# A fused attention, expert and MLP kernel: sums of a set's end moved and spread, one conversion moved forward

## The chip, the cores and the metric

The kernel runs on one core of one Trainium2 chip. Its engines are TensorE (PE in the profile, PEld its weight loads), VectorE (DVE), ScalarE (ACT), GpSimd (POOL) and SyncE (SP), which here only issues DMAs. Each engine works through its own instructions in order. The metric is the device time of one execution in microseconds.

## The reference, cut to what matters

```
attn = softmax(q_c @ k_c.T / 8) @ v_c               # chunks of 64, float32
x = attn, heads beside each other                   # 2304 tokens x 512
logits = x @ w_gate;  P = exp(logits - max)
8 times: P /= rows + eps;  P /= columns + eps;  P *= N / E
out = sum over 8 experts of P[:, e] * (relu(x @ w1[e]) @ w2[e])     # 512 -> 1024 -> 512
h = out @ w_in                                      # 512 -> 2048
return (h * clip(h + 3, 0, 6) / 6) @ w_out          # 2048 -> 512
```

Everything is float32 to the caller, but `w_in` and `w_out` arrive as float64, which the kernel turns into float32 with integer operations.

## The kernel before, in words

Every float32 factor is cut into a high and a low part (ScalarE rounds the high part, GpSimd or VectorE subtracts it for the low one), and each product is three TensorE passes over such parts. Large products are split further in the manner of Strassen and Winograd: seven products of half-size blocks in place of eight, with sums of blocks before (of weights, of x) and after (of results).

**Phase one** (to about 301 us) does the attention, the gate and expert 0. While it ends, the first weights of the next phase are loaded and cut.

**The steps.** The rest are 108 steps (`slots`), 28 for each of three token ranges ("sets" one to three, experts 1 to 7) and then 8 for each of the three ranges in the MLP (sets four to six). A step has seven positions, one for each product of `ORDER` (line 871 in the profile, results `ha`, `hb`, `hc`); between products TensorE does the second matrix product of an earlier step (line 1011 in sets one and two, lines 1098 and 1107 later). The rows read from the profile use line numbers of the kernel before.

**Side work.** Other work is put at a place (step, position) in a table: `at_slot` at a fixed one, `book` at the first position from a given one on at which the planner's costs of each engine stay under `CAP`. So the code's order, and with it each engine's order, comes out of this table. The side work that the change touches:

- The float64 conversion (`book_cv`): 32 tiles of seven VectorE instructions each (`cv_op`, lines 191 to 206), with a load before and a store after. 25 tiles stand in set one, 7 in set two.
- `book_ahead`: weight sums, cuts and stores of the MLP's first steps (experts' sets 28 to 31), in set two, through two buffers in turn.
- `book_x2`: cutting the MLP's input of a finished token range into parts, through two buffers in turn, and storing each part (`x2_keep`).
- Step 0's own second weights (`raw_load2(0)` and `w2_piece`), loaded and cut when step 0 begins; step 1's first weights (`w1_piece`) cut in step 0 with the low part on VectorE.

**Sums after, sets three to six.** A group of two steps makes seven results m = 1..7, each added by VectorE (line 1119) into its 768 columns of `accM`; in the first group of a set ScalarE writes them instead (line 1117). In a set's last group the seven are combined (`comb`, line 1066, VectorE, both operands and the result in SBUF) and four blocks are sent out (`block_out`). `MS` is the order in which results come, `y` counts the 14 half positions of a group. In a position the code of a step's own sums comes ahead of the side work and of the group's result.

```
    def acc_m(m):
        return ring["acc"][:, m - 1]

    COMB = {2: [(2, 1)], 5: [(3, 5)], 6: [(6, 1), (7, 6), (3, 6), (5, 7)], 4: [(4, 7)]}
```

So behind result 6 four combinations stand in a row, and in each set result m lies at the same place.

## Time and profile before

| | before |
|---|---|
| median of three runs | 2016.98 us (2009.76 to 2021.1) |
| the profiled execution | 2011.85 us |
| its span, first to last instruction | 2009.8 us |
| TensorE busy | 1942.4 us, 97% |
| VectorE busy | 1389.0 us, 69% |
| GpSimd busy | 1147.3 us, 57% |
| mean granted TensorE clock | 0.989 |

The profiled execution's own time is 2.05 us above its span, and 5.1 us under the median of the three runs. Busy time of TensorE is the sum of pipelined matmuls, so it also covers part of what is lost between them. The granted clock is a share of 2.4 GHz; 0.5 of it is 1.2 GHz.

### The profile page before, as it was taken

The page shows a single profiled execution, that of the slowest core. Times are in us where ns is not written, and L with a number is a line of the kernel's source. Part 1 is how long each engine was busy: PE and PEld are TensorE (multiplying, and loading weights), DVE is VectorE, ACT ScalarE, POOL GpSimd, SP SyncE. Part 2 cuts the span into 40 slices and gives each one's busy share as a digit, 9 for nine tenths or more (in the row PEclk, how much of TensorE's full clock was granted, in tenths as well). Part 3 has the DMA queues.
Part 4 walks back from the last instruction along what each step waited for, and adds up shares of the span by engine and source line. Part 5 has one row for each costly group of instructions (what it writes and reads, how often), then busy time and mean ns, then how long its engine had stood idle before and what let it go on. Part 6 is the DMA issues. An engine that isn't in the chain of part 4 may idle for free.

```text
span 2009.8 us, 33618 instructions
## 1 busy us (share of the span) xinstructions
PE 1942.4 (97%) x11709; PEld 1800.9 (90%) x11709; DVE 1389.0 (69%) x2278; ACT 795.6 (40%) x1586; POOL 1147.3 (57%) x997
## 2 busy tenths in 40 slices
PE   7999999999999999999989999999999999989998
PEld 6778787999999999998878999999999999989998
DVE  6554465788878854559775428778888877777767
ACT  3322224544444445444444434333333344444442
POOL 3221335776777755667666546667667645555443
PEclk8999999999999999999999999999999999999999
DMA  9856558777777779999999887899999998978874
GB/s 219 202 160 172 183 194 267 225 224 249 241 240 222 236 265 314 320 328 363 351 359 364 269 285 276 301 294 351 328 337 334 357 328 281 348 247 297 276 251 147
DMA packets 341704, 552.83 MB, mean 275 GB/s; under 512 B 47504, under 2 KB 171552, under 8 KB 341280
## 3 DMA queue, kind: packets, MB, share of 16 engines
q1 hardware_dynamic: 341536, 550.69, 82.7%
q8 instruction: 93, 1.52, 0.3%
q14 instruction: 75, 0.61, 0.1%
HBM read 365.97 MB, written 184.62 MB: 274 GB/s over the span
## 4 chain that ended last, share of the span: by engine, by line
PE 79%; DMA 7%; DVE 7%; POOL 3%; issue 2%; SPq 2%; ACT 2%; DVEq 0%; ACTq 0%; POOLq 0%
PE acc L1011 19%; PE hb L871 15%; PE ha L871 10%; PE o L1107 10%; PE hc L871 10%; PE o L1098 7%; PE h L546 3%; PE acc L580 3%; DMA wsc<-m 2%; DVE accM L1066 1%; POOL SS L788 1%; DMA q_None<-in_q_dram 1%; DVE accM L1119 1%; SPq L259 1%; DMA r<-in_moe_w_dram 1%
## 5 line engine op out<-in xcount | busy, mean ns | idle before, releaser
L1011 PE MATMUL acc<-W,H 128*128 128x512 f32 x2016 | 519.1, 392 | 10.0 <-POOL H L894 7.2
L1011 PEld LDWEIGHTS acc<-W,H 128*128 128x128 f32 x2016 | 376.0, 188 | 68.0 <-POOL H L894 9.8
L871 PE MATMUL hb<-X,W 128*128 128x384 f32 x1560 | 319.2, 339 | 0.9 <-DVE u L913 0.6
L788 POOL TENSOR_TENSOR W<-r,W 128x512 fp32r<-128x512 f32 x220 | 292.5, 1361 | 9.6 <-DMA r<-in_moe_w_dram 7.2
L871 PEld LDWEIGHTS hb<-X,W 128*128 128x128 f32 x1560 | 276.8, 189 | 13.3 <-DVE u L913 2.2
L871 PE MATMUL hc<-X,W 128*128 128x384 f32 x1200 | 243.6, 338 | 9.5 <-DVE H L888 8.9
L894 POOL TENSOR_TENSOR H<-u,H 128x384 fp32r<-128x384 f32 x112 | 121.1, 1081 | 195.7 <-ACT H L893 172.0
L871 PEld LDWEIGHTS hc<-X,W 128*128 128x128 f32 x1200 | 211.5, 188 | 22.0 <-DVE H L888 12.2
L871 PE MATMUL ha<-X,W 128*128 128x384 f32 x912 | 188.2, 341 | 15.4 <-ACT p L917 14.7
L913 DVE TENSOR_TENSOR u<-hb,p 128x384 f32<-128x384 f32 x216 | 119.6, 554 | 105.5 <-PE hb L871 92.3
L913 DVE TENSOR_TENSOR u<-hc,u 128x384 f32<-128x384 f32 x216 | 119.5, 553 | 101.1 <-PE hc L871 100.6
L871 PEld LDWEIGHTS ha<-X,W 128*128 128x128 f32 x912 | 161.9, 190 | 21.9 <-ACT p L917 16.2
L1119 DVE SCALAR_TENSOR_TENSOR accM<-o,accM 128x768 f32<-128x768 f32 x154 | 147.0, 955 | 48.7 <-PE o L1107 30.3
L892 ACT ACTIVATE u<-u 128x384 f32<-128x384 f32 x112 | 58.8, 525 | 265.7 <-DVE u L913 265.6
L1107 PE MATMUL o<-Hb,W2R 128*128 128x384 f32 x660 | 141.5, 337 | 0.2 <-DMA W2R<-wsc 0.2
L788 POOL TENSOR_TENSOR Hb<-u,Hb 128x384 fp32r<-128x384 f32 x93 | 103.4, 1113 | 59.4 <-ACT Hb L787 49.0
L1098 PE MATMUL o<-W2R,Hb 128*128 128x256 f32 x846 | 130.8, 285 | 0.0
L787 ACT ACTIVATE W<-r 128x512 fp32r<-128x512 f32 x224 | 119.7, 594 | 3.9 <-DMA r<-in_moe_w_dram 3.7
L1098 PEld LDWEIGHTS o<-W2R,Hb 128*128 128x128 f32 x846 | 119.3, 192 | 0.1
L1107 PEld LDWEIGHTS o<-Hb,W2R 128*128 128x128 f32 x660 | 117.7, 188 | 0.4 <-issue 0.4
L1107 PE MATMUL o<-Ha,W2R 128*128 128x384 f32 x516 | 111.7, 336 | 0.0
L546 PE MATMUL h<-xh,w 128*128 128x256 f32 (+1 forms) x384 | 108.5, 349 | 0.0
(190 smaller groups left out, 3578.7 us busy)
## 6 DMA issues: line engine op xcount, KB each, us to landing
W<-wsc SPq DMA_DIRECT2D x504, 256.0 KB, 4.6
W2R<-wsc SPq DMA_DIRECT2D x182, 512.0 KB, 5.3
wsc<-W SPq DMA_DIRECT2D x28, 1792.0 KB, 7.3
r<-in_moe_w_dram SPq DMA_DIRECT2D x112, 256.0 KB, 7.3
wsc<-SS SPq DMA_DIRECT2D x28, 1024.0 KB, 5.9
wsc<-m SPq DMA_DIRECT2D x48, 512.0 KB, 5.6
wsc<-W SPq DMA_DIRECT2D x28, 768.0 KB, 5.4
x2sc<-m SPq DMA_DIRECT2D x42, 384.0 KB, 4.4
```

What stands on the lines that cost most here:

```text
L546: nc.tensor.matmul(out=hps[:, :n], lhsT=w[:, a, kk, :], rhs=xx[:, kk, :], start=(kk == 0 and a == 0 and xx is xh), stop=(kk == KD - 1 and ...
L580: nc.tensor.matmul(out=o[:, :n] if turned else o, lhsT=w[:, a, c] if turned else hx[:, c], rhs=hx[:, :n] if turned else w[:, a, :], start= ...
L787: nc.scalar.activation(out=hi, in_=r, func=AF.Copy)
L788: lo_eng.tensor_tensor(out=lo, in0=r, in1=hi.bitcast(F32), op=ALU.subtract)
L871: nc.tensor.matmul(out=ps[:, :HN], lhsT=W1t[s.b][:, wo, a, kl, :], rhs=x[:, b, kl, :], start=(start and kl == 0 and a == 0 and b == 0), st ...
L892: nc.scalar.activation(out=src, in_=src, func=AF.Relu)
L894: nc.gpsimd.tensor_tensor(out=lo, in0=src, in1=hf, op=ALU.subtract)
L913: nc.vector.tensor_tensor(out=o, in0=ps[b][:, :HN], in1=x, op=ALU.add)
L1011: nc.tensor.matmul(out=o, lhsT=s.Hs[:, fi, hx, t * 128:(t + 1) * 128], rhs=w[:, 0::3, a, :] if fi == 0 else w[:, 1:3, a, :], start=(s.j % ...
L1098: nc.tensor.matmul(out=o[:, t * 256:(t + 1) * 256], lhsT=hs[q][:, b, t * 128:(t + 1) * 128], rhs=w[:, q, a, :], start=(q, a, b) == mm[0], ...
L1107: nc.tensor.matmul(out=ps[:, d, :HN], lhsT=w[:, q, a, d * 128:(d + 1) * 128], rhs=hs[q][:, b, :], start=(q, a, b) == mm[0], stop=(q, a, b) ...
L1119: nc.vector.scalar_tensor_tensor(out=dst, in0=src, scalar=sc, in1=dst, op0=ALU.mult, op1=ALU.add)
```

## The change

What it does, by places in the diff:

1. A set's end: the combinations are bound to half positions `y` instead of results. Five stay on VectorE, three go to GpSimd; (6, 1) is replaced by (7, 1) and (3, 1), which together with (7, 6) and (3, 6) give the same sums. The outputs of blocks 3, 5 and 4 are issued at y = 13 and 14 (the next group's first). `home` puts a new set's results where the old set's come free in the order `FREED`.
2. The float64 conversion: all 32 tiles in set one, from position 9 instead of 12, without the positions left free between instructions, with `CAP` of VectorE at 2.1 instead of 1.95.
3. `book_ahead` in set two starts 4 positions sooner, with 3 positions between cuts instead of 2.
4. `x2_keep` is issued 3 positions behind its cut instead of 2.
5. Step 0's second weights are loaded in phase one (pool `raw2` opens there, `Pb` moves to the other side of SBUF) and cut from position 1; two of step 1's four first-weight cuts have the low part on GpSimd.

```
-    COMB = {2: [(2, 1)], 5: [(3, 5)], 6: [(6, 1), (7, 6), (3, 6), (5, 7)], 4: [(4, 7)]}
-    DONE = {2: [2], 6: [3, 5], 4: [4]}
-    COMB_LAST = {2: [(2, 1)], 6: [(6, 1), (3, 6)], 7: [(7, 6), (4, 7)], 5: [(3, 5), (5, 7)]}
-    DONE_LAST = {2: [2], 5: [3, 5], 4: [4]}
+    V, G = nc.vector, nc.gpsimd
+    ENDS = {
+        MS: ({5: [(G, 2, 1)], 7: [(V, 3, 5)], 9: [(V, 7, 1), (G, 3, 1)],
+              11: [(V, 7, 6), (G, 3, 6)], 12: [(V, 5, 7)], 13: [(V, 4, 7)]},
+             {7: [2], 13: [3, 5], 14: [4]}),
+        MS_LAST: ({3: [(G, 2, 1)], 7: [(V, 6, 1), (G, 3, 6)], 9: [(V, 7, 6), (V, 4, 7)],
+                   11: [(G, 3, 5), (V, 5, 7)]},
+                  {5: [2], 12: [3, 5], 13: [4]}),
+    }
+    FREED = (1, 6, 7, 2, 3, 5, 4)
...
+        if groups[-1].last:
+            home = {m: home[f] for m, f in zip(MS, FREED)}
...
-    def acc_m(m):
-        return ring["acc"][:, m - 1]
-
-    def comb(d, a):
-        nc.vector.tensor_tensor(out=acc_m(d), in0=acc_m(a), in1=acc_m(d), op=ALU.add)
+    def acc_m(g, m):
+        return ring["acc"][:, g.home[m]]
+
+    def comb(g, eng, d, a):
+        eng.tensor_tensor(out=acc_m(g, d), in0=acc_m(g, a), in1=acc_m(g, d), op=ALU.add)
...
+        if y == 0 and n and groups[n - 1].last:
+            close_group(groups[n - 1], 14)
         if g.last:
-            cb, dn = (COMB_LAST, DONE_LAST) if g.ms is MS_LAST else (COMB, DONE)
-            for pair in cb.get(m, ()):
-                comb(*pair)
-            for x in dn.get(m, ()):
-                block_out(g, x)
+            close_group(g, y)
+
+    def close_group(g, y):
+        sums, outs = ENDS[g.ms]
+        for x in sums.get(y, ()):
+            comb(g, *x)
+        for m in outs.get(y, ()):
+            block_out(g, m)
...
-            opened("r", "Pb", 2, "right")
             opened("rr", "raw1", 2, "right")
+            opened("rr", "raw2", 2, "right")
...
+        add(s + 8, 2, raw_load2, 0)
...
-        for name, bufs in (("tmp", 2), ("W11", 1), ("XE", 1), ("M", 1)):
+        for name, bufs in (("tmp", 2), ("W11", 1), ("XE", 1), ("M", 1), ("Pb", 2)):
...
-        raw_load2(0)
...
-        CAP = {"DVE": 1.95, "ACT": 2.4, "POOL": 2.6}
+        CAP = {"DVE": 2.1, "ACT": 2.4, "POOL": 2.6}
...
-                    at_slot(0, z, w1_piece, s, z, nc.vector)
+                    at_slot(0, z, w1_piece, s, z, nc.vector if z > 1 else nc.gpsimd)
...
-            h = book_cuts(g + (1 if s.i else 4), g + 7, [(w2_piece, s, z) for z in range(2)])
+            h = book_cuts(g + 1, g + 7, [(w2_piece, s, z) for z in range(2)])
...
-                    if x in (2, 4):
-                        g += 1
                 at_slot(0, g + 1, cv_keep, i)
-                g = g + 1 if two else max(g + 1, h + 4)
+                g = g if two else max(g + 1, h + 4)
...
-        CV1 = 25
-        g = book_cv(12, list(range(CV1)), True)
+        CV1 = len(cv_list)
+        g = book_cv(9, list(range(CV1)), True)
...
-                at_slot(0, g + 2, x2_keep, p, kl, o)
+                at_slot(0, g + 3, x2_keep, p, kl, o)
...
-        g0 = done[0] + 6
-        book_cv(g0, list(range(CV1, len(cv_list))), False)
+        g0 = done[0] + 2
...
-        g = book_ahead(g0, range(NEXP, FAR), 2, 2)
+        g = book_ahead(g0, range(NEXP, FAR), 2, 3)
```

What this makes of the engines' order, at three places. First VectorE in step 10 of set one, from the step's first sum (`u_10<-hb`) to the weight sums of step 12 (`r_12`); the conversion's instructions are those on `m`. Before:

```order
L913 TENSOR_TENSOR u_10_5063<-hb_5056,p_10_5036 128x384
L198 SCALAR_TENSOR_TENSOR m<-m 128x512
L888 SCALAR_TENSOR_TENSOR H_5035<-ha_5028,H_5035 128x384
L201 TENSOR_SCALAR m<-m 128x512
L913 TENSOR_TENSOR u_10_5102<-hb_5056,p_10_5036 128x384
L770 TENSOR_TENSOR r_12_4986<-r_12_4986 128x256 x3
```

and now:

```order
L913 TENSOR_TENSOR u_10_5101<-hb_5094,p_10_5076 128x384
L204 SCALAR_TENSOR_TENSOR m<-m 128x512
L206 SCALAR_TENSOR_TENSOR m<-m 128x512
L888 SCALAR_TENSOR_TENSOR H_5075<-ha_5068,H_5075 128x384
L191 TENSOR_SCALAR m<-m 128x512
L194 TENSOR_SCALAR m<-m 128x512
L196 TENSOR_SCALAR m<-m 128x512
L913 TENSOR_TENSOR u_10_5145<-hb_5094,p_10_5076 128x384
L770 TENSOR_TENSOR r_12_5022<-r_12_5022 128x256 x3
```

Between the same two sums stand five conversion instructions instead of two, and three of them follow each other directly ahead of the sum that reads `hb` again. In the whole step there are 13 instead of 9, and the last conversion stands in step 22 instead of 26 (of those in set one).

Second VectorE at the end of set three, from the last sum on `hc` before the fourth combination to the differences of step 85 (`t_85`); `accM<-o` is a result added, `accM<-accM` a combination. Before:

```order
L913 TENSOR_TENSOR u_85_15789<-hc_15799,u_85_15789 128x384
L1119 SCALAR_TENSOR_TENSOR accM<-o_5_15792,accM 128x768
L1066 TENSOR_TENSOR accM<-accM 128x768 x4
L949 SCALAR_TENSOR_TENSOR u_85_15789<-u_15810,u_85_15789 128x384
L913 TENSOR_TENSOR p_85_15727<-hb_15739,p_85_15727 128x384
L949 SCALAR_TENSOR_TENSOR p_85_15727<-u_15837,p_85_15727 128x384
L913 TENSOR_TENSOR u_85_15749<-hc_15799,u_85_15749 128x384
L1119 SCALAR_TENSOR_TENSOR accM<-o_6_15840,accM 128x768
L1066 TENSOR_TENSOR accM<-accM 128x768
L949 SCALAR_TENSOR_TENSOR u_85_15749<-u_15857,u_85_15749 128x384
L994 TENSOR_TENSOR t_85_15785<-u_85_15749,t_85_15785 128x384
```

and now:

```order
L913 TENSOR_TENSOR u_85_15791<-hc_15801,u_85_15791 128x384
L1127 SCALAR_TENSOR_TENSOR accM<-o_5_15794,accM 128x768
L1075 TENSOR_TENSOR accM<-accM 128x768
L949 SCALAR_TENSOR_TENSOR u_85_15791<-u_15812,u_85_15791 128x384
L913 TENSOR_TENSOR p_85_15726<-hb_15739,p_85_15726 128x384
L1075 TENSOR_TENSOR accM<-accM 128x768
L949 SCALAR_TENSOR_TENSOR p_85_15726<-u_15835,p_85_15726 128x384
L913 TENSOR_TENSOR u_85_15749<-hc_15801,u_85_15749 128x384
L1127 SCALAR_TENSOR_TENSOR accM<-o_6_15838,accM 128x768
L1075 TENSOR_TENSOR accM<-accM 128x768
L949 SCALAR_TENSOR_TENSOR u_85_15749<-u_15856,u_85_15749 128x384
L994 TENSOR_TENSOR t_85_15787<-u_85_15749,t_85_15787 128x384
```

One combination is left behind result 6 where four were; another now stands behind the sum into `p_85`, and the one behind result 4 has stayed. GpSimd has got, in the same stretch, between the low parts that it cuts (`Ha`, `Hb`):

```order
L788 TENSOR_TENSOR Hb<-u_84_15641,Hb 128x384
L1075 TENSOR_TENSOR accM<-accM 128x768
L788 TENSOR_TENSOR Hb<-t_85_15787,Hb 128x384
L788 TENSOR_TENSOR Hb<-p_84_15579,Hb 128x384
L1075 TENSOR_TENSOR accM<-accM 128x768
L788 TENSOR_TENSOR Hb<-u_85_15791,Hb 128x384
```

These are (3, 1) and (3, 6), which GpSimd did not have before; (2, 1) stands five rows ahead of them.

Third GpSimd at step 0, from the last cut of step 0's first weights (`W_0` from `r_0`, before its number changes) on; `H` are the low parts of step 0's own results. Before:

```order
L788 TENSOR_TENSOR W_0_3045<-r_0_3046,W_0_3045 128x256
L894 TENSOR_TENSOR H_3672<-u_0_3716,H_3672 128x384
L788 TENSOR_TENSOR W_0_3738<-r_0_3661,W_0_3738 128x2x256
L894 TENSOR_TENSOR H_3672<-p_0_3673,H_3672 128x384
L788 TENSOR_TENSOR W_0_3738<-r_0_3661,W_0_3738 128x2x256
L894 TENSOR_TENSOR H_3672<-u_0_3688,H_3672 128x384
```

and now:

```order
L788 TENSOR_TENSOR W_0_3045<-r_0_3046,W_0_3045 128x256
L788 TENSOR_TENSOR W_1_3662<-r_1_3049,W_1_3662 128x2x256 x2
L788 TENSOR_TENSOR W_0_3692<-r_0_3451,W_0_3692 128x2x256 x2
L894 TENSOR_TENSOR H_3672<-u_0_3721,H_3672 128x384
L894 TENSOR_TENSOR H_3672<-p_0_3673,H_3672 128x384
L894 TENSOR_TENSOR H_3672<-u_0_3688,H_3672 128x384
```

The two cuts of the second weights (`W_0_3738` before, `W_0_3692` now) stood between step 0's results and now stand ahead of them, and two cuts for step 1 (`W_1`) have come from VectorE.

## Rows read from the trace of the kernel before

**Rows 1.** The page: TensorE's total, Vector's share in 40 slices.

```profile
PE 1942.4 (97%) x11709; PEld 1800.9 (90%) x11709; DVE 1389.0 (69%) x2278; ACT 795.6 (40%) x1586; POOL 1147.3 (57%) x997
...
DVE  6554465788878854559775428778888877777767
```

**Rows 2.** Whom TensorE waited for, whole execution: sum, times, longest.

```profile
PE ha L871 <- ACT p L917: 14.7, 5, 5.3
PE hc L871 <- DVE H L888: 8.9, 8, 2.8
PE acc L1011 <- POOL H L894: 7.2, 5, 2.8
...
PE acc L1011 <- POOL W L788: 2.0, 1, 2.0
```

**Rows 3.** Four stretches: length; busy PE, PEld, DVE, ACT, POOL; clock.

```profile
315.00:322.00 7.00, 5.63 (x15) 4.85 (x16) 0.56 (x1) 2.02 (x5) 6.67 (x7) 0.52 0.99 366
380.20:442.50 62.30, 62.30 (x313) 56.55 (x313) 50.82 (x74) 27.73 (x56) 44.53 (x37) 1.00 0.75 237
897.00:1105.00 208.00, 192.64 (x946) 169.73 (x945) 152.37 (x220) 88.87 (x177) 148.05 (x117) 1.00 1.01 361
1776.00:1780.00 4.00, 3.57 (x15) 3.57 (x16) 3.28 (x4) 2.60 (x5) 3.92 (x3) 0.57 0.98 299
```

**Rows 4.** Waits of ScalarE from 897 to 1105 us.

```profile
ACT m L787 <- DMA wsc<-m: 60.2, 19, 7.9
```

**Rows 5.** TensorE's order, 1007 to 1013 us: start, us, what.

```profile
1007.40 1.22 PE L871 MATMUL hb<-X,W 128*128 128x384 f32 x6
1008.46 1.52 PE L1011 MATMUL acc<-W,H 128*128 128x512 f32 x6
1012.44 1.31 PE L871 MATMUL hc<-X,W 128*128 128x384 f32 x6 [2.46 <-DVE H L888]
```

**Rows 6.** Vector's groups by line, 380.2 to 442.5 us.

```profile
L770 DVE TENSOR_TENSOR r<-r 128x256 f32<-128x256 f32 x16 | 12.4, 792 | 0.1
...
L204 DVE SCALAR_TENSOR_TENSOR m<-m 128x512 f32<-128x512 uint32 x4 | 4.2, 1051 | 0.0
...
L191 DVE TENSOR_SCALAR m<-m 128x512 uint32<-128x512 uint32 x4 | 1.8, 461 | 0.0
```

**Rows 7.** One Vector line, 335 to 733 us: ns shortest/median/longest.

```profile
L770 DVE TENSOR_TENSOR r<-r x96: 408/416/1502, 342.4 to 704.5; 128x256 f32<-128x256 f32 x96
```

**Rows 8.** The same for a line that reads PSUM.

```profile
L913 DVE TENSOR_TENSOR u<-hb,p x52: 543/558/559, 337.2 to 731.7; 128x384 f32<-128x384 f32 x52
```

**Rows 9.** GpSimd in order of time from 300 us.

```profile
311.88 1.02 POOL L894 TENSOR_TENSOR H<-u,H 128x384 fp32r<-128x384 f32 x1 [19.78 <-DMA r<-in_moe_w_dram]
```

**Rows 10.** Vector in order of time at a set's end.

```profile
1634.90 3.69 DVE L1066 TENSOR_TENSOR accM<-accM 128x768 f32<-128x768 f32 x4
...
1640.27 0.85 DVE L949 SCALAR_TENSOR_TENSOR p<-u,p 128x384 f32<-128x384 f32 x1 [0.74 <-ACT u L944]
...
1642.49 1.15 DVE L1066 TENSOR_TENSOR accM<-accM 128x768 f32<-128x768 f32 x1
```

**Rows 11.** TensorE in order of time: the stops behind ScalarE.

```profile
1645.81 1.42 PE L871 MATMUL ha<-X,W 128*128 128x384 f32 x5 [3.54 <-ACT p L917]
...
1738.64 1.65 PE L871 MATMUL ha<-X,W 128*128 128x384 f32 x4 [2.11 <-ACT p L917]
...
1776.43 1.97 PE L871 MATMUL ha<-X,W 128*128 128x384 f32 x5 [5.35 <-ACT p L917]
```

**Rows 12.** ScalarE in order of time, third set.

```profile
1737.28 0.52 ACT L634 ACTIVATE m<-m 128x384 fp32r<-128x384 f32 x1 [2.80 <-DMA x2sc<-m]
```

**Rows 13.** GpSimd's groups of the whole execution (page).

```profile
L894 POOL TENSOR_TENSOR H<-u,H 128x384 fp32r<-128x384 f32 x112 | 121.1, 1081 | 195.7 <-ACT H L893 172.0
```

**Rows 14.** Vector in order of time at the end.

```profile
2003.04 1.95 DVE L1066 TENSOR_TENSOR accM<-accM 128x768 f32<-128x768 f32 x2
2004.90 0.95 DVE L1119 SCALAR_TENSOR_TENSOR accM<-o,accM 128x768 f32<-128x768 f32 x1
```

More of the change, by code (lines that the diff above doesn't have):

```diff
@@ L1048, in chunk_attention_moe_mlp @@
             ab=(a, b), mlp=s.mlp, p=s.p, at=s.i + 2, first=s.j == 0,
-            last=b.i + 1 in ends, ms=MS_LAST if b is slots[-1] else MS,
+            last=b.i + 1 in ends, ms=MS_LAST if b is slots[-1] else MS, home=home,
         ))
+        if groups[-1].last:
+            home = {m: home[f] for m, f in zip(MS, FREED)}
     ring = {}
@@ L1071, in block_out @@
             nc.sync.dma_start(
-                out=xraw[:, :, i, j, :], in_=acc_m(m).rearrange("p (k n) -> p k n", k=2)
+                out=xraw[:, :, i, j, :], in_=acc_m(g, m).rearrange("p (k n) -> p k n", k=2)
             )
@@ L1410, in chunk_attention_moe_mlp @@
             opened("a", name, bufs, "left")
-        opened("rr", "raw2", 2, "right")
         opened("rr", "sum2", 1, "right")
```

30 lines of the change are left out of this document (15 added, 15 removed).

## The prediction

> **What bounds the kernel now.** I read the page first, then TensorE's waits, then stretches of the span, and last single engines in order of time where TensorE stopped. TensorE is busy for 97% of the span, while VectorE's share varies between 4 and 8 tenths [rows 1]. What can be won is therefore what TensorE loses at its stops, and most of the steps lose nothing: the 62.30 us from 380.2 to 442.5 hold four steps with TensorE busy for all of them, 15.58 us a step and 15.58 / 7 = 2.23 us a position [rows 3]. Here VectorE is busy for 50.82 us, so it has 11.5 us free per four steps. The stops lie at three kinds of places.
>
> *Step 0.* TensorE waits 2.0 us for the low part of a second weight [rows 2], and some smaller waits for results' low parts (1.8 us together, a part of the 7.2 and 8.9 us of [rows 2]) come before it. GpSimd itself had stood for 19.78 us behind a load of weights [rows 9], so its queue runs late. From 315 to 322 the granted clock is 0.52, 1.2 GHz against the 2.4 GHz of a normal stretch [rows 3]: another 7.0 x 0.48 = 3.4 us. Together 7.2 us.
>
> *Set two while the MLP's weights are prepared.* From 897 to 1105 us TensorE is busy for 192.64 of 208.00 us [rows 3]: 15.4 us in ten stops, the longest 2.8 us, nearly all named "low part of a result, GpSimd or VectorE" [rows 2]. Behind them stands ScalarE, which in that stretch waits 60.2 us in 19 waits for a store out of one of `book_ahead`'s two buffers, at most 7.9 us [rows 4]. ScalarE's next cut of a result is queued behind such a wait, the low part behind the cut, and the product that reads it behind that. One stop in order of time: two products begin 1.06 us apart, the next one 3.98 us later, of which 2.46 us are idle [rows 5].
>
> *The set ends.* TensorE stops 3.54 us at the end of set three and 5.35 us at the end of set four [rows 11]; set five's end repeats the first (the five waits on `p` of 14.7 us [rows 2], less the three of [rows 11], leave 3.7 us for it and a small one; I take 3.5). At 1776 to 1780 the clock is 0.57 [rows 3], a further 4.0 x 0.43 = 1.7 us. ScalarE's `p` comes late because VectorE does four combinations in one go, 3.69 us, and a fifth of 1.15 us right ahead of the next step's differences [rows 10]. All three ends cost 12.4 + 3 x 1.7 = 17.5 us.
>
> A last stop of 2.11 us stands alone at 1738.64 [rows 11]: ScalarE had waited 2.80 us for a store of `book_x2` [rows 12].
>
> **The change part by part.** The sum is made against the profiled execution, 2011.85 us (span 2009.8 and 2.05 us around it).
>
> *Step 0.* The second weights' loads move ahead of the first results, their two cuts with them, so the 2.0 us wait has no ground left, and the low clock that follows a stop goes if the stop goes: 2.0 + 3.4 = 5.4 us. Against it, three loads are now on SP's queue ahead of three other issues of phase one, and GpSimd gets two cuts that VectorE did. Below: the 2.0 us alone. Above: all 7.2. **Term: -5.5** (-2 to -7).
>
> *Set two.* With 3 positions between cuts the way from a buffer's store to its next use grows from 2 positions, 2 x 2.23 = 4.5 us, to 4, 8.9 us, and the longest wait was 7.9 us [rows 4]. That would be above every store seen. The conversion's loads and stores leave this stretch as well, and its work starts 4 positions sooner. If all waits go, 15.4 us come back; a wait that stays behind another queue keeps some. **Term: -15** (-12 to -17; a whole failure is a rival below).
>
> *Set ends.* Behind result 6 stand now one combination and not four. VectorE still does five per end, but ahead of the differences only three, spread: 4.84 us before, 3 x 0.92 = 2.8 us now, and the 0.74 us that it stood for `u` behind them [rows 10] goes too: it gets there up to 2.8 us sooner. Three go to GpSimd. It has no such sum in the trace; its nearest row is the low part, 1081 ns for 384 columns [rows 13], so about 2.2 us for 768 (an estimate from that row). What such a sum costs VectorE is shown by a line that adds two operands from SBUF: 416 ns in the median and 1502 at most, and 792 in the mean of the dense stretch [rows 6, 7], while a line with one operand in PSUM takes 543 to 559 ns whatever runs beside it [rows 8]. So one of VectorE's SBUF sums can be held by 1.1 us, and by all of the 2.2 us at worst. Per end that leaves between 0.6 and 2.8 us; taking 2.0 of it, three times: **-6** (0 if the stretch eats it, -17.5 if every stop and its low clock go).
>
> [...]
>
> *`book_x2` one position later.* In the third set a buffer is used again 4 positions on, so its store now has one position less before reuse. The wait that already costs 2.11 us there [rows 11, 12] grows by up to 2.23 us. Other sets use the buffers more slowly, and there the slack covers it. **+2** (0 to +4).
>
> *The tail.* Two combinations and an addition ended the kernel on VectorE, 1.95 + 0.95 us [rows 14]. Now (3, 5) is on GpSimd, about 2.2 us by the estimate above, and (5, 7) must wait until it has read result 5, with the last addition queued behind it. **+1** (0 to +2).
>
> *Set one.* The conversion goes from 28 to 41 instructions per four steps (32 tiles of seven, 224, over about 21.7 steps). Its seven lines take from 461 to 1051 ns [rows 6], 23.5 us for 28, so 0.84 us in the mean; 13 more are 10.9 us in 11.5 free ones [rows 3, 6]. On average they fit, but VectorE is then full to the last per cent, and where three stand in a row, the low part that `hb` or `hc` waits for stands behind 2.5 us of them. Over 21.7 / 4 = 5.4 such cycles the loss is 0 if all fits and 15 us if an instruction costs 1.05 us (13 x 1.05 = 13.7, 2.2 too much, and once more for irregularity); nearer the first, as products come two positions after their cuts. **+4** (0 to +15).
>
> *At nothing:* `home` and `FREED` (an address, no instruction; ScalarE writes a new set's results where the old are out already, and TensorE covers it, busy through), the later outputs (store queues idle then; one would cost its landing, of the size of [rows 4], only if its columns were reused at once).
>
> Sum: -5.5 - 15 - 6 + 2 + 1 + 4 = -19.5, that is 1992.4 us on the profiled execution. The four known times (three runs and the profiled one) have a mean of 2014.9, 3.1 us above it, which I add: **1995 us**.
>
> **The rivals** (times with those 3 us).
> 1. *All stops vanish.* 7.2 + 15.4 + 17.5 + 2.1 = 42.2 us: 1973. For it: each is a short wait behind a named instruction. Against it: set ends need over 5 us and get 2.8.
> 2. *GpSimd's sums hold VectorE for their whole length.* The set ends give nothing, the tail costs 2: 1995 + 6 + 1 = 2002. For it speak the 1502 ns [rows 7].
> 3. *Set two keeps its stops,* because the stores wait for a queue and not for time: the 60.2 us [rows 4] stay, with 4 positions between. 1995 + 15 = 2010, no change to be told. Against it: 7.9 us was the longest.
> 4. *The other side: VectorE becomes the bound of set one.* If an added conversion costs 1.5 us, as the held sum does [rows 7], then 13 x 1.5 = 19.5 us meet 11.5 free ones; 8.0 x 5.4 = 43 us in place of 4: 1995 + 39 = 2034. It decides from the price at which the loss is 23.5 us, 13p = 11.5 + 23.5 / 5.4, p = 1.22 us. For it: the fullest stretch has 45 us of GpSimd beside VectorE [rows 3]. Against it: that 0.84 was measured beside the same GpSimd.
>
> **How the numbers follow.** Chances: the forecast 0.55, rival 1 0.13, rival 2 0.12, rivals 3 and 4 0.10 each. The forecast's own range, terms partly summed, is 1983 to 2005. For 8 in 10 the range takes in rival 1 and rival 2 and rival 3's middle: 1972 to 2012; rival 4 stays out. A change of 0.5% (10 us) is about what this measurement can tell; below 2007 counts as faster. Forecast, rivals 1 and 2 lie there but for 0.03 and 0.02: 0.75, and 0.03 of rivals 3 and 4 where gains elsewhere carry them, so faster 0.78. Same 0.13 (rival 3 and those edges), slower 0.09.
>
> **What would show it.** Step 0: no wait of the second product for a weight's low part, clock 1.0 behind it. Set two: ScalarE's 60.2 us of waits for stores nearly gone, ten stops of TensorE gone. Set ends: stops of 1 to 3 us at the three places, the row of four combinations split, VectorE's SBUF sums longer where GpSimd's stand beside. `book_x2`: a stop of 2 to 4 us in the third set. Set one: steps still 15.58 us; a window of four steps above 62.30 with TensorE waiting for `H` from VectorE would show rival 4, and make the prediction wrong.

## The result and the profile after

The changed kernel takes 2028.66 us in the median of 12 runs (2023.03 to 2033.28), the kernel before 2016.51 us (12 runs, 2009.76 to 2021.1). The ratio is 1.0063, with a 95% interval of 1.0048 to 1.0078: 12 us slower, where 1995 us and a gain were forecast. The profiled execution of the changed kernel has a span of 2021.8 us, 12.0 us above that of the kernel before.

Line numbers of the kernel after differ from those before in the result's part alone: 1107, 1098, 1119, 1066 are now 1116, 1107, 1127, 1075; 1117 is 1125. First the page: TensorE's total, and VectorE's busy tenths in 40 slices.

```profile
PE 1944.4 (96%) x11709; PEld 1798.7 (89%) x11709; DVE 1388.0 (69%) x2267; ACT 794.3 (39%) x1586; POOL 1182.9 (59%) x1011
...
DVE  6554466899999734444454528778888877877766
```

TensorE's work is the same as in [rows 1]. In set one VectorE's slices 9 to 13 have gone from 7 and 8 to 9, which is 90% or more; in set two its slices 19 to 21 from 9, 7 and 7 to 4, 4 and 5. Then TensorE's waits over the whole execution, as sum, times, longest:

```profile
PE ha L871 <- ACT p L917: 18.1, 6, 4.8
PE hb L871 <- DVE u L913: 13.7, 17, 1.9
PE hc L871 <- DVE H L888: 5.7, 4, 2.1
```

The waits of [rows 2] for low parts from GpSimd (7.2 us in five) and for a weight (2.0 us) are gone. A wait that cost 0.6 us before is now the second, 13.7 us in 17, and its releaser is VectorE. The waits for `p` grew from 14.7 to 18.1 us.

Where the 12 us lie is read from when the first product of each step starts (TensorE in order of time). A second profile of the kernel before, taken later, stands beside it:

| from the first product of ... | before | before, again | changed |
|---|---|---|---|
| the start (phase one) | 301.23 | 306.79 | 304.80 |
| steps 0 and 1 | 32.23 | 29.90 | 28.46 |
| steps 2 to 26 (set one) | 389.75 | 389.76 | 416.57 |
| steps 38 to 49 (set two) | 206.56 | 206.59 | 187.56 |
| steps 85 and 86 (end of set three) | 35.67 | 36.78 | 35.79 |
| steps 92 and 93 | 34.55 | 32.73 | 35.83 |
| step 94 (end of set four) | 21.87 | 23.01 | 22.31 |
| steps 101 and 102 (end of set five) | 35.37 | 36.50 | 36.45 |
| step 107 to the end | 36.88 | 36.89 | 37.95 |

Phase one differs by 5.6 us between two executions of one program, so its 3.6 us say nothing of the change. Of the rest set one lost 26.8 us and set two won 19.0 us; everything else together comes to 0.6 us. The loss in set one is itself from one profile: four of the runs below have the same code there, and with theirs it is 25.5 to 31.1 us.

Two stretches of the changed kernel, with the columns of [rows 3]: four steps of set one (13 to 16), and steps 38 to 49.

```profile
522.39:587.93 65.54, 63.62 (x314) 55.97 (x313) 63.80 (x88) 27.71 (x56) 49.12 (x37) 1.00 0.73 232
924.38:1111.94 187.56, 187.56 (x937) 169.55 (x937) 88.25 (x159) 84.37 (x168) 128.85 (x109) 1.00 1.00 345
```

Four steps that took 62.30 us take 65.54, with VectorE busy for 63.80 of them: it has 1.7 us left, where it had 11.5. In set two TensorE is busy for the whole stretch, VectorE for 88 us (152 of 208 before [rows 3]), and ScalarE's wait for the stores out of the two buffers [rows 4] does not appear any more.

VectorE's groups by line from 333 to 687 us, four of them (the last operation of the conversion, the weight sums, then the conversion's sixth and first operation), with count, busy us, mean ns and the idle time before them:

```profile
L206 DVE SCALAR_TENSOR_TENSOR m<-m 128x512 f32<-128x512 f32 x31 | 41.5, 1340 | 0.7
L770 DVE TENSOR_TENSOR r<-r 128x256 f32<-128x256 f32 x84 | 41.2, 506 | 0.5
...
L204 DVE SCALAR_TENSOR_TENSOR m<-m 128x512 f32<-128x512 uint32 x31 | 32.9, 1060 | 13.0 <-DMA scr_in<-m 9.6 <-DMA scr_out<-m 2.8
...
L191 DVE TENSOR_SCALAR m<-m 128x512 uint32<-128x512 uint32 x31 | 25.8, 834 | 0.5
```

L191 took 461 ns before [rows 6] and takes 834; L770 has fallen from 792 to 506. All seven conversion lines together take 1.012 us an instruction (219.6 us for 217 in this stretch), against 0.829 us in steps 2 to 26 of the kernel before (143.4 us for 173).

What an instruction waits for can be read from the trace one by one. Of the 218 conversion instructions in steps 2 to 26 of the changed kernel 139 take over 0.2 us more than the shortest of their line. Each of these 139 ends one such shortest time after the end of a GpSimd instruction (to within 0.15 us), as if it had begun only then, and of the 39 that no GpSimd instruction runs beside none is longer. Their time above the shortest is 104.5 us together. In the kernel before 72 of 172 are longer, by 48.8 us together.

The row of L204 shows something else that the prediction did not have. VectorE waits 12.4 us in eight waits, up to 3.7 us, for a store of the conversion to leave; in the kernel before no such wait is in the trace. L204 writes the buffer that the tile's result is stored from, and there is one such buffer: without the positions left free, the next tile comes to it before the last store has landed.

How the hold reaches TensorE is seen at 559 us, first in VectorE's order, then in GpSimd's and TensorE's:

```profile
558.27 1.13 DVE L194 TENSOR_SCALAR m<-m 128x512 uint32<-128x512 uint32 x1
559.43 1.41 DVE L196 TENSOR_SCALAR m<-m 128x512 uint32<-128x512 uint32 x1
560.87 1.67 DVE L198 SCALAR_TENSOR_TENSOR m<-m 128x512 uint32<-128x512 uint32 x1
562.47 0.54 DVE L913 TENSOR_TENSOR u<-hb,p 128x384 f32<-128x384 f32 x1
```

```profile
558.01 1.11 POOL L894 TENSOR_TENSOR H<-u,H 128x384 fp32r<-128x384 f32 x1 [0.79 <-ACT H L893]
559.08 7.18 POOL L788 TENSOR_TENSOR W<-r,W 128x512 fp32r<-128x512 f32 x5
```

```profile
563.07 1.31 PE L871 MATMUL hb<-X,W 128*128 128x384 f32 x6 [0.42 <-DVE u L913]
```

Three conversion instructions stand in a row ahead of the sum that `hb` waits for. They take 1.13, 1.41 and 1.67 us, 4.2 us together, where a position is 2.23 us long. GpSimd is busy beside all three. So the sum starts late, and TensorE stops for 0.42 us. Of the 17 stops on this sum 15 lie between 345 and 684 us, and three on `hc` beside them, up to 2.1 us each. Four of these 18 stops (5.2 us of 16.6) come 1.6 to 3.0 us behind one of VectorE's waits for a store; no run separates their share.

At the end of set three, GpSimd's combinations, VectorE's next to them, and TensorE's stop:

```profile
1638.40 2.56 POOL L1075 TENSOR_TENSOR accM<-accM 128x768 f32<-128x768 f32 x1
...
1643.18 2.56 POOL L1075 TENSOR_TENSOR accM<-accM 128x768 f32<-128x768 f32 x1
```

```profile
1637.56 1.70 DVE L1075 TENSOR_TENSOR accM<-accM 128x768 f32<-128x768 f32 x1
...
1642.75 1.30 DVE L1075 TENSOR_TENSOR accM<-accM 128x768 f32<-128x768 f32 x1
1643.97 2.20 DVE L949 SCALAR_TENSOR_TENSOR u<-u,u 128x384 f32<-128x384 f32 x1
```

```profile
1653.42 2.15 PE L871 MATMUL ha<-X,W 128*128 128x384 f32 x6 [4.33 <-ACT p L917]
```

These two GpSimd combinations take 2.56 us each (the shortest of the twelve takes 1.80). While a GpSimd instruction runs, a VectorE instruction with two operands from SBUF takes longer, until that one ends: the two combinations took 1.70 and 1.30 us where 0.92 was the mean in [rows 10], beside low parts that GpSimd cuts, and the instruction at 1643.97, beside the second GpSimd combination, 2.20 us instead of 0.55. The stop on `p` is 4.33 us, 3.54 before [rows 11].

At step 0, ScalarE's copy of expert 0's last results, GpSimd's four weight cuts, and VectorE beside them:

```profile
307.35 0.73 ACT L599 ACTIVATE ev<-acc 128x256 f32<-128x256 f32 x2 [2.69 <-PE cp L511]
```

```profile
309.05 5.50 POOL L788 TENSOR_TENSOR W<-r,W 128x512 fp32r<-128x512 f32 x4 [13.38 <-DVE u L913]
```

```profile
309.30 1.08 DVE L520 TENSOR_SCALAR scs<-scs 128x8 f32<-128x8 f32 x1
...
310.65 1.10 DVE L525 TENSOR_TENSOR P<-P,scr 128x144 f32<-128x144 f32 x1
...
312.13 1.29 DVE L788 TENSOR_TENSOR W<-r,W 128x512 fp32r<-128x512 f32 x1
```

The two stops on the second weights are gone. TensorE now waits for `p` (1.20 us), which stands behind the copy at 307.35, and longer for VectorE (1.38, 0.36 and 1.23 us, where 0.40, 0.82 and 0.61 were lost to it before). The wait for `p` is no sure mark of the change: it is 0.44 us in the second profile of the kernel before, and 0.14 us in one of the runs below with the changed step 0 (that with GpSimd relieved). The longer ones come from VectorE's instructions: L520 took 0.17 us before and takes 1.08, L525 0.31 and takes 1.10, the cut 0.68 and takes 1.29, all while GpSimd cuts four pieces in a row.

### The profile page after: what moved, and what is told of

It reads as the page before. It is cut to its first block, busy times and chain, and to the rows that moved or that the text cites. A ratio compares the mean times of both kernels' runs of the same rounds, so it can differ in the third digit from the quotient of the medians.

```text
span 2021.8 us, 33668 instructions
## 1 busy us (share of the span) xinstructions
PE 1944.4 (96%) x11709; PEld 1798.7 (89%) x11709; DVE 1388.0 (69%) x2267; ACT 794.3 (39%) x1586; POOL 1182.9 (59%) x1011
## 4 chain that ended last, share of the span: by engine, by line
PE 71%; DVE 15%; DMA 6%; issue 4%; ACT 1%; SPq 1%; POOL 1%; POOLq 0%; DVEq 0%; ACTq 0%
PE acc L1011 16%; PE hb L871 13%; PE o L1116 10%; PE hc L871 9%; PE ha L871 9%; PE o L1107 7%; PE acc L580 3%; PE h L546 3%; DVE u L913 2%; DMA scr_out<-m 1%; DVE m L204 1%; DVE r L770 1%; DVE m L194 1%; DMA st<-in_moe_w_dram 1%; DVE accM L1127 1%
## 5 line engine op out<-in xcount | busy, mean ns | idle before, releaser
L871 PE MATMUL hb<-X,W 128*128 128x384 f32 x1560 | 320.1, 340 | 13.8 <-DVE u L913 13.7
L788 POOL TENSOR_TENSOR W<-r,W 128x512 fp32r<-128x512 f32 x222 | 302.8, 1393 | 18.1 <-DVE u L913 13.4
L871 PE MATMUL ha<-X,W 128*128 128x384 f32 x912 | 188.4, 342 | 18.8 <-ACT p L917 18.1
L788 POOL TENSOR_TENSOR Hb<-u,Hb 128x384 fp32r<-128x384 f32 x93 | 103.7, 1116 | 49.8 <-ACT Hb L787 44.3
```

What stands on the lines that cost most here:

```text
L788: lo_eng.tensor_tensor(out=lo, in0=r, in1=hi.bitcast(F32), op=ALU.subtract)
L871: nc.tensor.matmul(out=ps[:, :HN], lhsT=W1t[s.b][:, wo, a, kl, :], rhs=x[:, b, kl, :], start=(start and kl == 0 and a == 0 and b == 0), st ...
```

## The experiments

The main theory after the result: GpSimd's instructions hold VectorE's instructions on SBUF (not those that read PSUM, [rows 8]), so each instruction added to VectorE in set one costs more than its own time, and the same holds for the combinations moved to GpSimd. The rival: VectorE's own amount and order of work alone.

**Conversion spread over all of set one.**

```diff
-                    g = book(g, cv_op, i, x, dve=c)
+                    g = book(max(g, 9 + (7 * n + x) * 4 // 5), cv_op, i, x, dve=c)
```

> The changed kernel with its 224 conversion instructions spread evenly over set one, 0.8 of a position apart (35 in four steps, the last in step 26, instead of 41 and step 22). Theory A, VectorE is simply over-full in set one (41 x 1.01 us and the rest ask for more than the 62.3 us of four steps): 35 x 0.9 us fit nearly, the 26.8 us that steps 2 to 26 lost against the kernel before shrink below 6, and the whole is 20 to 26 us shorter than the changed kernel. Theory B, it is not the amount but several conversion instructions standing ahead of one sum: at one or two a position with the weight sums between them the stops stay in part, and at least 12 of the 26.8 us remain.

Measured: 2005.62 us, ratio to the kernel before 0.9955 (0.9940 to 0.9970). Steps 2 to 26 take 400.15 us: 10.4 of the 26.8 us remain, between the two expectations. The stretch from 380 to 660 us:

```profile
380.00:660.00 280.00, 276.38 (x1374) 249.49 (x1373) 245.47 (x353) 123.01 (x251) 200.40 (x157) 0.99 0.76 245
```

VectorE has 34.5 of 280 us free and TensorE still loses 3.6, in stops of 0.6 to 1.8 us on `hb` every 64 us. One of them, VectorE first:

```profile
469.05 0.69 DVE L204 SCALAR_TENSOR_TENSOR m<-m 128x512 f32<-128x512 uint32 x1 [3.71 <-DMA scr_out<-m]
469.78 1.64 DVE L206 SCALAR_TENSOR_TENSOR m<-m 128x512 f32<-128x512 f32 x1
471.34 0.54 DVE L913 TENSOR_TENSOR u<-hb,p 128x384 f32<-128x384 f32 x1
```

```profile
471.94 1.68 PE L871 MATMUL hb<-X,W 128*128 128x384 f32 x6 [1.83 <-DVE u L913]
```

So the amount counts. What is left is not a matter of amount or rows alone: each of the six stops in steps 2 to 26 comes 2.9 to 4.0 us behind a wait of VectorE of 2.2 to 3.7 us for a store of the conversion, and behind the wait stands an instruction that GpSimd holds. No run takes these waits away at this density.

**Conversion as before, the new distances in set two kept.**

```diff
-        CV1 = len(cv_list)
-        g = book_cv(9, list(range(CV1)), True)
+        CV1 = 25
+        g = book_cv(12, list(range(CV1)), True)
...
+        book_cv(done[0] + 6, list(range(CV1, len(cv_list))), False)
         g0 = done[0] + 2
```

with the old free positions and the old cap.

> The changed kernel with the conversion as it was before (25 tiles in set one, 7 in set two, the old distances and the old cap of 1.95), but with the new distances of the weight preparation in set two. Set one: steps of 15.58 us again, about -26 us against the changed kernel by either theory. Set two: if the third position between cuts is what removed ScalarE's 60.2 us of waits for stores, they stay below 10 us and 897 to 1105 loses under 3 us; if it was that the conversion's seven tiles left this stretch (their loads, stores and VectorE work), at least 10 of the 19 us gained there are lost again.

Measured: 2000.47 us, ratio 0.9939 (0.9922 to 0.9956). Set one is back at 389.76 us. Steps 38 to 49 take 189.56 us, 17.0 of the 19.0 us that were won. ScalarE's waits for stores in that stretch:

```profile
ACT m L787 <- DMA wsc<-m: 8.4, 5, 3.4
```

8.4 us in place of 60.2 [rows 4]: `book_ahead`'s own new places are what cured set two (the third position between cuts and the sooner start, which this run keeps both and does not separate); that the conversion left it is worth 2.0 us.

**All combinations on VectorE, at the same places.**

```diff
-        MS: ({5: [(G, 2, 1)], 7: [(V, 3, 5)], 9: [(V, 7, 1), (G, 3, 1)],
-              11: [(V, 7, 6), (G, 3, 6)], 12: [(V, 5, 7)], 13: [(V, 4, 7)]},
+        MS: ({5: [(V, 2, 1)], 7: [(V, 3, 5)], 9: [(V, 7, 1), (V, 3, 1)],
+              11: [(V, 7, 6), (V, 3, 6)], 12: [(V, 5, 7)], 13: [(V, 4, 7)]},
...
```

(The last set's table, `MS_LAST`, is changed in the same way.)

> The changed kernel with the three GpSimd combinations of each set end given to VectorE, at the same half positions. Theory A, a GpSimd sum of 2.56 us holds VectorE's sums with two SBUF operands for its whole length (2.20 us for one that takes 0.55): VectorE reaches the differences of the next step 2 to 3 us sooner, the stops of 4.33, 4.79 and 4.28 us at the three set ends fall to 1 to 3 us, the tail loses the 1.98 us that VectorE waits for GpSimd, and the whole is 5 to 9 us shorter. Theory B, VectorE is late there by its own work: five to eight combinations cost it 0.94 us each, the stops become as long as in the kernel before (3.5 to 5.4 us) or longer, and only the tail's 1 us is won.

Measured: 2025.79 us, ratio 1.0057 (1.0043 to 1.0071), which can't be told from the changed kernel's 1.0063 (1.0048 to 1.0078). The three set ends take 92.61 us together (changed 94.55, before 92.91 and 96.29), the tail 36.89. The stops are 3.33, 4.03 and 3.02 us, above theory A's 1 to 3 and below those of the kernel before. Neither theory holds alone: without GpSimd's combinations VectorE has eight of its own, which are long here too, since GpSimd's low parts run beside them:

```profile
1639.88 2.65 DVE L1075 TENSOR_TENSOR accM<-accM 128x768 f32<-128x768 f32 x2
...
1645.29 2.17 DVE L1075 TENSOR_TENSOR accM<-accM 128x768 f32<-128x768 f32 x2
...
1648.32 0.94 DVE L1075 TENSOR_TENSOR accM<-accM 128x768 f32<-128x768 f32 x1
...
1651.91 1.43 DVE L1075 TENSOR_TENSOR accM<-accM 128x768 f32<-128x768 f32 x1
```

Six combinations, 7.2 us, stand ahead of the differences.

**GpSimd relieved in set one.** ScalarE writes the low parts of the weights as a copy; the subtraction is left out. (The expectation says sets one and two; set two reads these weights ready from memory, so the edit works in set one alone.)

```diff
+        if lo_eng is None:
+            nc.scalar.activation(out=lo, in_=r, func=AF.Copy)
+            return
         lo_eng.tensor_tensor(out=lo, in0=r, in1=hi.bitcast(F32), op=ALU.subtract)
...
```

(The lines left out name the weights of steps 2 to 27.)

> The changed kernel, but in sets one and two the low parts of the weights are written by ScalarE as a plain copy (the subtraction is left out), so GpSimd only cuts results there; VectorE has the same instructions in the same density, 41 conversion instructions in four steps. Theory A, the conversion is dear because GpSimd's instructions hold VectorE's: its mean falls from 1.01 us to 0.6 to 0.75, VectorE has time left, and most of the 26.8 us lost in steps 2 to 26 is gone (20 us or more shorter than the changed kernel). Theory B, VectorE's own work and its order do it: the mean stays over 0.9 us and the steps stay at 15.6, 17.1 and 17.2 us.

Measured: 2003.56 us, ratio 0.9945 (0.9930 to 0.9961). Steps 2 to 26 take 391.75 us: 24.8 of the 26.8 us are gone, with every VectorE instruction in its place. The same three groups and a stretch of 65 us (DVE is the third of the busy times, POOL the fifth):

```profile
L770 DVE TENSOR_TENSOR r<-r 128x256 f32<-128x256 f32 x89 | 35.8, 418 | 0.6
...
L206 DVE SCALAR_TENSOR_TENSOR m<-m 128x512 f32<-128x512 f32 x32 | 22.2, 693 | 0.7
...
L191 DVE TENSOR_SCALAR m<-m 128x512 uint32<-128x512 uint32 x31 | 14.6, 471 | 0.5
```

```profile
515.00:580.00 65.00, 65.00 (x328) 59.03 (x327) 48.42 (x93) 40.35 (x82) 12.79 (x12) 1.00 0.82 267
```

L206 falls from 1340 to 693 ns and L191 from 834 to 471. The mean of the seven lines is 0.61 us. GpSimd is busy for 12.8 us of 65 instead of 49 of 65.5, and TensorE never stops in this stretch. VectorE's waits for the conversion's stores are still there, 23.4 us in eleven, and behind them comes TensorE's only stop of over 0.3 us in set one, 1.17 us. This settles it: the price is GpSimd's, and the waits for stores cost nearly nothing without it.

**The store of `book_x2` 2 positions behind its cut again.**

```diff
-                at_slot(0, g + 3, x2_keep, p, kl, o)
+                at_slot(0, g + 2, x2_keep, p, kl, o)
```

> The changed kernel with book_x2's store again 2 positions behind its cut instead of 3. Theory A, the position taken from the time between store and reuse made the third set's stop longer: the stop at step 92 (3.1 to 3.5 us in the changed kernel and its variants) falls to about 2.1 us, and the stops of 1.06 and 0.95 us that came in step 93 go: 2 to 3 us in steps 92 and 93. Theory B, those stops come from the store's own landing or from another queue: they stay within 0.5 us.

Measured, one run: 2027.04 us. TensorE's stops in steps 92 and 93:

```profile
1751.26 1.44 PE L871 MATMUL ha<-X,W 128*128 128x384 f32 x6 [1.79 <-ACT p L917]
...
1775.40 1.34 PE L871 MATMUL hb<-X,W 128*128 128x384 f32 x6 [1.06 <-DVE u L913]
...
1778.72 1.32 PE L871 MATMUL hc<-XE,W 128*128 128x384 f32 x6 [0.93 <-DVE u L913]
```

The first falls from 3.10 to 1.79 us, as theory A has it, but this profile wins no time by it: step 92 takes 18.37 us (18.16 in the changed kernel). Over all profiles here it takes 18.2 to 20.9 us in the eight with 3 positions, 19.9 in the mean, and 16.7 to 18.7 us in the six with 2, 17.6 in the mean, so the position costs some 2.3 us. The other two stops stay, and are not `book_x2`'s. They are not GpSimd's either: step 93 takes 17.5 us here and 17.98 and 17.96 us in the two runs that have these combinations on VectorE (the one above and that with late combinations), but 15.8 to 16.0 in the kernel before and the joined ones. What only the latter are without is the pair (7, 1) and (3, 1), which stands in step 93; that it is the cause is not shown.

**The old share of the conversion, three at a time.**

```diff
-                    g = book(g, cv_op, i, x, dve=c)
+                    g = max(g, 9 + (7 * n + x) // 3 * 3)
+                    at_slot(0, g, cv_op, i, x)
```

(25 tiles in set one, 7 in set two.)

> The changed kernel with the old share of the conversion in set one (25 tiles, 28 instructions in four steps, as in the kernel before), but placed three at a time in every third position instead of one or two a position; seven tiles follow in set two. Theory A, the loss in set one comes from the amount (VectorE beside GpSimd has no time for 41 of them in four steps): with 28 steps 2 to 26 stay at 389.8 us or lose under 3 us. Theory B, three in a row ahead of a sum are enough by themselves: each third position loses some tenths of a us, 10 to 27 us in all, as in the changed kernel.

Measured, one run: 2038.59 us. Steps 2 to 26 take 402.28 us, 12.5 us more than with the same instructions one or two at a time: theory B, near its lower end. None of VectorE's waits here is for a store of the conversion, so the rows of three do it without them; an instruction takes 0.93 us in the mean (0.83 at one or two a position). In set two the edit puts all seven instructions of a tile into one position, an extreme that was not meant and shows the mechanism best. VectorE, and then TensorE:

```profile
979.43 1.51 DVE L191 TENSOR_SCALAR m<-m 128x512 uint32<-128x512 uint32 x1
...
985.37 1.48 DVE L201 TENSOR_SCALAR m<-m 128x512 uint32<-128x512 uint32 x1
986.89 0.69 DVE L204 SCALAR_TENSOR_TENSOR m<-m 128x512 f32<-128x512 uint32 x1
```

```profile
988.83 1.65 PE L871 MATMUL hb<-X,W 128*128 128x384 f32 x4 [6.81 <-DVE u L913]
```

Seven instructions from 979.43 to 988.22 (five of them held at 1.4 to 1.6 us, the last two free at 0.69) and a stop of 6.81 us on the sum behind them. Steps 38 to 49 take 215.09 us.

**Step 0's second weights loaded sooner.**

```diff
-        add(s + 8, 2, raw_load2, 0)
+        add(s + 3, 2, raw_load2, 0)
```

> The changed kernel with step 0's second weights loaded five half steps sooner in phase one, ahead of the queue that its last stores stand in. Theory A, these loads delay the store out of ScalarE's copy of expert 0's results, and with it the first p of step 0: ScalarE's wait for that store falls from 2.7 to 3.8 us to 1.5 us as before, and TensorE's stop on ha in step 0 (1.2 to 2.3 us) goes; the three stops on VectorE behind it (1.4, 0.4 and 1.2 us) stay, since they come from GpSimd's four weight cuts in a row. Theory B, ScalarE's wait has to do with the 1792 KB store of the first weights alone: the stop on ha stays over 1 us.

Measured, one run: 2024.71 us. ScalarE's copy:

```profile
307.50 0.70 ACT L599 ACTIVATE ev<-acc 128x256 f32<-128x256 f32 x2 [3.93 <-DMA asc_t<-ev]
```

The wait is still 3.93 us and the stop on `ha` 2.41 us. Theory A of this run falls; what delays that store stays open. The three stops on VectorE behind it, which both theories let stand, shrink to one of 0.74 us; why is not shown.

**The late combinations.**

```diff
-        MS: ({5: [(G, 2, 1)], 7: [(V, 3, 5)], 9: [(V, 7, 1), (G, 3, 1)],
-              11: [(V, 7, 6), (G, 3, 6)], 12: [(V, 5, 7)], 13: [(V, 4, 7)]},
-             {7: [2], 13: [3, 5], 14: [4]}),
+        MS: ({5: [(V, 2, 1)], 7: [(V, 3, 5)], 9: [(V, 7, 1), (V, 3, 1)],
+              15: [(V, 7, 6), (V, 3, 6)], 16: [(V, 5, 7), (V, 4, 7)]},
+             {7: [2], 15: [3], 16: [5, 4]}),
...
-        if y == 0 and n and groups[n - 1].last:
-            close_group(groups[n - 1], 14)
+        if n and groups[n - 1].last:
+            close_group(groups[n - 1], 14 + y)
```

> The changed kernel with all combinations of a set's end on VectorE, and the four that need result 6 moved behind the last differences of the old set's last step (half positions 15 and 16, the next group's second and third), with the outputs behind them; the old columns are free before the new results 3 and 2 come. Theory A, what costs at a set's end is that sums with two SBUF operands, GpSimd's or VectorE's, stand ahead of the differences that ScalarE's p is queued behind: the stops of 4.3, 4.8 and 4.3 us fall below 1 us each and the low clock behind them goes, 12 to 18 us. Theory B, the step at the boundary itself (other weights, ScalarE writing the first results) makes the stop: at least 2.5 us of each stay.

(`MS_LAST` goes to VectorE here too, at its old places.) Measured: 2015.26 us, ratio 1.0006 (0.9993 to 1.0020), 0.57% or some 11.5 us below the changed kernel's ratio. The set ends take 32.02, 17.65 and 31.72 us, 13.2 us less together, and the tail 1.1 us less. The clock in these three stretches is 1.00, where the changed kernel has 0.95, 0.85 and 0.91. The waits for `p` in the whole execution:

```profile
PE ha L871 <- ACT p L917: 6.0, 5, 2.9
```

6.0 us in place of 18.1, half of it the one at step 92. Theory A, though a stop of 1.44 us on `hb` has come in step 94.

**Joined.** The conversion as before, the store 2 positions behind its cut, the set ends late with (6, 1) back in place of (7, 1) and (3, 1):

```diff
...
+        MS: ({5: [(V, 2, 1)], 7: [(V, 3, 5)], 14: [(V, 6, 1)], 15: [(V, 7, 6), (V, 3, 6)],
+              16: [(V, 5, 7), (V, 4, 7)]},
+             {7: [2], 15: [3], 16: [5, 4]}),
...
```

> The changed kernel with what the runs spoke for: the conversion as before (25 tiles in set one), book_x2's store 2 positions behind its cut, and the set ends with all combinations on VectorE and five of the seven behind the last differences. If the stages add up without touching each other: set one 389.8 us, set two's stretch 189.6 us, the set ends as in the run with late combinations (14 us under the kernel before together), steps 92 and 93 under 35 us. That is 26 to 30 us below the kernel before, some 1.3 to 1.5%. Rival: the late combinations collide with the cuts of the third set's MLP input, whose stop at step 92 grows and takes back over 5 us.

Measured: 1982.04 us (1981.57 to 1984.34), ratio 0.9845 (0.9830 to 0.9861): 1.5% below the kernel before, some 31 us where 26 to 30 were expected. Set one 390.20 us, steps 38 to 49 189.73, the set ends 31.02, 18.64 and 31.11, steps 92 and 93 32.87, so the rival falls. The last four combinations at the end of set three, and TensorE around them:

```profile
1628.49 2.63 DVE L1075 TENSOR_TENSOR accM<-accM 128x768 f32<-128x768 f32 x2
...
1631.52 2.65 DVE L1075 TENSOR_TENSOR accM<-accM 128x768 f32<-128x768 f32 x2
```

```profile
1635.15 1.31 PE L871 MATMUL hb<-XE,W 128*128 128x384 f32 x6 [0.79 <-DVE u L913]
...
1643.70 1.30 PE L871 MATMUL ha<-X,W 128*128 128x384 f32 x6
```

These four cost VectorE 5.3 us, more than the 4.84 us of the five in [rows 10]. But they stand behind the second and the third difference, and ScalarE's `p` is queued behind its cut of the first: TensorE loses 0.79 us on one product and none on `p`, which stopped it for 3.54 us. The end of set four still stops it for 0.91 us on `p` and 2.39 us on `hb`.

**Step 1's first weights cut on VectorE again**, in the joined kernel:

```diff
-                    at_slot(0, z, w1_piece, s, z, nc.vector if z > 1 else nc.gpsimd)
+                    at_slot(0, z, w1_piece, s, z, nc.vector)
```

and **step 0 wholly as before**, in the joined kernel: the same line, the pools as before, and

```diff
-        add(s + 8, 2, raw_load2, 0)
...
+        raw_load2(0)
...
-            h = book_cuts(g + 1, g + 7, [(w2_piece, s, z) for z in range(2)])
+            h = book_cuts(g + (1 if s.i else 4), g + 7, [(w2_piece, s, z) for z in range(2)])
```

> The joined kernel with all four low parts of step 1's first weights on VectorE again, while the second weights stay loaded in phase one. Theory A, step 0's three stops on VectorE (1.4, 0.4 and 1.2 us) come from GpSimd's four weight cuts in a row, which hold VectorE's SBUF sums: with two of them left the stops shrink by over 1 us, steps 0 and 1 together take 1 to 3 us less than in the joined kernel. Theory B, VectorE is late there by its own work: two more cuts of 0.7 us make the stops longer, by 1 us or more.

> The joined kernel with step 0 wholly as in the kernel before (second weights loaded and cut when step 0 begins, pools as before). If the edit of step 0 is worth what it showed, steps 0 and 1 take 32.2 us again, 1 to 4 us more than in the joined kernel. Rival: the loads moved into phase one lengthen it (301.2 us in the one profile of before, 303.7 to 310.1 in those of the changed kernel and its variants): then phase one is 2 to 6 us shorter here, and the whole is no longer than the joined kernel, or shorter.

Measured: 1982.82 us, ratio 0.9854 (0.9834 to 0.9874), and 1985.66 us, ratio 0.9858 (0.9839 to 0.9878), which can't be told from the joined kernel's. With the cuts on VectorE the stops on VectorE in step 0 fall from 1.38, 0.37 and 1.24 us to 0.32 and 1.31, 1.4 us less, as theory A has it; but steps 0 and 1 take 31.82 us for 29.29, since the clock was 0.50 from 310 to 318 us there and 1.00 in the joined kernel. So the time that theory A forecast did not come. With the old step 0 they take 32.39 us, at a clock of 0.79 from 318 to 326 us; phase one is 304.64 us, inside the spread of the others, so the rival falls.

**The kernel before, once more,** with no edit.

> The kernel before, unchanged, for a second profile of it. If phase one's length varies from execution to execution by itself, it differs here by over 1.5 us from the 301.2 us of the first profile; if it is the changed step 0 that lengthens it, it stays between 300 and 302.5 us. The later stages repeat within 0.5 us each, or the differences read from single profiles are worth less than taken.

Measured, one run: 2016.63 us. Phase one takes 306.79 us for 301.23: it varies by itself. Set one and two repeat within 0.03 us, the set ends only within 1.1 us each, and steps 0 and 1 differ by 2.3 us, steps 92 and 93 by 1.8 us.

## Why the prediction was wrong, step by step

**Set one: +4 was +26.8 us. This step failed, and with it the sign.** The prediction priced an added instruction at 0.84 us, the mean measured at the old density, and found that 13 fit into 11.5 us of free time. The price was not a property of the instruction. Nearly all of it above the 0.6 us that the run without GpSimd's weight cuts shows is waiting for GpSimd, and that grew with the number of instructions that met one: 1.01 us, for all 41. Four steps therefore ask 41 x 1.012 - 28 x 0.829 = 18.3 us more, of which the weight sums give back 16 x (785 - 506) ns = 4.5 us: 13.8 us into 11.5 free ones, 2.3 us too much, or 12 us over 5.4 such cycles. The prediction's upper bound, with 1.05 us for the 13 added ones, has nearly this sum (2.2 us too much); its forecast stayed near nothing, "as products come two positions after their cuts". The second half of the mistake was to count free time in the mean. The bound allowed some 3 us "for irregularity"; with no instruction added, the old ones in threes lost 12.5 us, and the denser table stands in threes too. The two halves are about as large as what was lost, though the runs don't show that they simply add. And a term is missing: 12.4 us of VectorE's free time went into waits for the conversion's own stores, which the prediction did not ask about. They stop TensorE only where GpSimd is busy as well, and how much of the 26.8 us is theirs stays open. Rival 4 named the place and the mechanism; its price of 1.22 us from which it decides was too high, because it too counted the mean alone.

The Trainium skill's rule ("SBUF — State Buffer", "Who interferes with whom") bears on this step. It says that besides instructions with two SBUF inputs also one-input ones, when they run in a two-port fast form, contend with GpSimd for a shared pair of ports. The trace agrees in kind: L191, with one input, takes between 426 and 1408 ns in the changed kernel's set one, and 471 in the mean where GpSimd is light; that it runs in such a form no run here shows. The prediction reckoned with a hold by GpSimd for the sums at the set ends [rows 6, 7], and for the conversion only in rival 4, at a chance of 0.10.

**Set two: -15 was -19.0.** The mechanism was right: the store has 4 positions, ScalarE's waits are gone, and 17.0 us come without the conversion's leaving. (The stops in this stretch are twelve, seven and five by releaser, not the ten of the prediction; their sum is right.) The term was mis-sized because it took the idle time of the stretch, 15.4 us, for the loss: the twelve steps were 19.0 us longer than they are without stops (12 x 15.63 us). Here the idle time between products understated what the stops cost; where the other 3.6 us were is not shown.

**Set ends: -6 was nothing** (94.55 us now and 92.9 to 95.7 in the six other profiles with these ends, 92.91 and 96.29 before). The prediction took 2.0 of 2.8 us per end as won, with a held sum at 1.1 us. GpSimd's combination is 2.56 us at the place shown (2.2 was estimated), and it holds an instruction of VectorE's ahead of the differences that ScalarE's `p` waits for by 1.65 us. So rival 2's result came, by its mechanism only in part: with no combination on GpSimd the ends were not clearly shorter (92.61 us). What helps is not the engine but the place: with the last four of eight behind the differences named above, the combinations on VectorE gain 13 us.

**`book_x2`: +2 was some +2.3** in step 92, in the means over all profiles (-0.5 and +1.4 in the changed one against the two of before); the stop itself went from 2.11 (1.67 again) to 3.10, and back to 1.79 when the position was given back. Its mechanism and its size were right. Step 93 lost a further 1.7 us, for which the prediction had no term. **Tail: +1 was +1.1,** with VectorE waiting 1.98 us for GpSimd's sum:

```profile
2015.77 0.96 DVE L1075 TENSOR_TENSOR accM<-accM 128x768 f32<-128x768 f32 x1 [1.98 <-POOL accM L1075]
```

**Step 0: -5.5 was -1.4 to -3.8.** The 2.0 us wait did go. The 3.4 us of low clock were wrongly charged to it, as the second profile of before has the same stop and no low clock (below). And with four cuts in a row on GpSimd the smaller stops on VectorE, 1.8 us before, became 3.0 us, by the same hold as in set one. The prediction had "GpSimd gets two cuts that VectorE did" among what speaks against the gain, without asking what VectorE does beside them.

## What to carry to other kernels

Price an instruction that is added to VectorE by what GpSimd does beside it: where GpSimd is busy for 7 tenths of the time, one that takes 0.4 to 0.7 us alone took 0.8 to 1.3 in the mean here, and free time in the mean says little, since a row of three in front of one sum that TensorE waits for stops it even where a fifth of VectorE's time is free. Denser work also comes sooner to its own buffers: look whether its stores have landed by then. A transfer between engines doesn't relieve VectorE if the receiver holds it. First look for what stands ahead of the waited-for instruction without need, and put it behind: that moved 13 us here, when the change of engine moved none.

## What the hardware showed that had not been expected

The low clock at step 0 comes and goes with one and the same program. In the first profile of the kernel before it is 0.52 from 315 to 322 us [rows 3], around the end of TensorE's stop of 2.01 us at 316.37; the second has the same stop of 2.01 us at 322.24 and this stretch around it (the last three figures are clock, DMA share and GB/s):

```profile
320.00:328.00 8.00, 5.99 (x29) 5.11 (x29) 0.85 (x2) 3.68 (x9) 7.61 (x7) 1.00 0.96 351
```

The clock there is 1.00. So what this stop costs in clock can't be read from a single profile. Between the two, phase one differs by 5.6 us and steps 0 and 1 by 2.3 us, while set one repeats to 0.01 us.
